# Numerator of the first half in SBUF, and y tiles grown one half at a time, in a fused attention and two-FFN kernel

## The chip, the cores and the metric

The kernel runs on one core of one Trainium2 chip. The metric is the device time of one execution in microseconds (us), lower is better; the figure for a kernel is the median of its runs.

## The reference

Attention over pooled keys and values, then a dense layer with a rational activation, then a routed layer in which each token goes to one of eight experts under a capacity limit:

```python
k_p = k.reshape(B, H, Sp, pool, D).mean(axis=3)          # pool = 8, Sp = 72
v_p = v.reshape(B, H, Sp, pool, D).mean(axis=3)
scores = scale * np.matmul(q, k_p.transpose(0, 1, 3, 2))
attn = softmax(scores)                                     # B = 8, H = 8, S = 576, D = 64
x = matmul(attn, v_p) as [4608 tokens, 512]
h = x @ w_in                                               # 512 -> 2048
P = a[0] + a[1] * h + a[2] * h2 + a[3] * h3
Q = 1.0 + np.abs(b[0]) * np.abs(h) + np.abs(b[1]) * h2
g = P / (Q + 1e-06)
y = g @ w_out                                              # 2048 -> 512
order = np.argsort(-(y @ w_gate).flatten())                # greedy: 576 tokens to each expert
out[mask] = np.maximum(y[mask] @ w1[e], 0.0) @ w2[e]       # 512 -> 1024 -> 512
```

## The kernel before

The 4608 tokens are 18 blocks of 256. Every float32 operand of a matmul is split into a high and a low part (`xh`/`xl`, `wih`/`wil`, `mg` high and low), and a product is three matmuls.

**Stages.** The dense layer is done in two halves of the 2048 hidden units. In the first half (`half` 0) attention is mixed in: units of scores (L560), softmax (L564 to L585), transposes (L595) and products with v (L613 to L616) make the next block's x while the blocks before it go through the dense layer. The second half (`half` 1) reads x back from DRAM. Then tokens are routed and the experts run (L1820 to L1863).

**A step.** One step is 256 hidden units of one block, or 128 hidden units of a pair of blocks: 512 columns in either case. There are 72 steps in each half. `mm_h` (L701) fills a PSUM bank `ph` with h. `act1` and `act2` work on 128x512 elements: ACT makes |h| (`ms`, L716), a3 h + a2 (`w`, L717) and the first term of Q (`q`, L719); DVE makes w h (L721) and then w = (w + a1) h (L722), POOL or DVE q |h|; ACT makes 1/Q by Ln and Exp (`mr`, L734 and L736). DVE then makes the high part of g (L737), a remainder `t` of it (L739, from q and the high part; L741, from w), and POOL the low part t/Q (L353, the line of a helper). In this kernel L722 writes w back into the bank `ph`, so that L737 and L741 read it there and the bank is held until L741 has ended.

**y.** `mm_y` multiplies g by `woh` and `wol` for one tile `tt` of 128 tokens. A tile is two PSUM banks, `g` = 0 and 1, of 260 columns each (256 of y, and 4 of the router's logits). The first tile of a part (all steps of one block or pair) grows step by step: after each step its matmuls go into both banks (L805 and L806 for the high part, L803 for the low). The other tiles are made when the part has all its steps, in `turn_y`. `y_out` then moves a finished tile out.

**Order.** PSUM has eight banks (`pa0` to `pa7`), which attention, `ph`, y and the preparation of weights share. Nothing is ordered by hand: each operation is recorded with an engine, a planned duration, what it reads and writes, and a list scheduler (`Order.run`) plays it through with the banks as a resource that is taken at an operation's start and freed when its last user ends. The order that comes out is the program, and each engine keeps to it. `w`, `q` have three buffers in turn (`mw`/`mq`, two of which are called `mwq` in the trace).

Of the kernel before, what the change touches and what calls it, by code (L numbers as in the profile page):

```python
# [18 lines left out]
ALU = mybir.AluOpType  # L19
# [4 lines left out]
B, H, S, D = 8, 8, 576, 64  # L24
# [7 lines left out]
NB = NT // BLK  # L32
# [266 lines left out]
class Kern:  # L299
# [408 lines left out]
    def act1(self, st):  # L708

        nc, op, i = self.nc, self.op, st["i"]  # L710
        ph = st["ph"]
        hk = [(ph, 0)]
        w, q, s = self.mw[i % 3], self.mq[i % 3], self.ms[i % 2]
        st["w"], st["q"] = ph, q
        N = 2 * BLK
        op("Act", c_act(N), lambda: nc.scalar.activation(s(), ph(), AF.Abs), r=hk, w=[s])  # L716
        op("Act", c_act(N, 0, 2), lambda: nc.scalar.activation(w(), ph(), AF.Identity, scale=self.a3(), bias=self.a2()),  # L717
           r=hk + self.sk, w=[w])
        op("Act", c_act(N, 1, 2), lambda: nc.scalar.activation(q(), s(), AF.Identity, scale=self.b1a(), bias=self.b0a()),  # L719
           r=[s] + self.sk, w=[q])  # L720
        op("DVE", c_tt(N), lambda: nc.vector.tensor_tensor(w(), w(), ph(), op=ALU.mult), r=hk, w=[w])  # L721
        op("DVE", c_stt(N), lambda: nc.vector.scalar_tensor_tensor(  # L722
            ph(), w(), self.a1(), ph(), op0=ALU.add, op1=ALU.mult), r=[w], w=hk)
        self.tt(N, q, q, s, ALU.mult, r=[s], w=[q])

    def act2(self, st):

        nc, op, i = self.nc, self.op, st["i"]
        w, q, r, t = st["w"], st["q"], self.mr[i % len(self.mr)], self.mt[i % MTB]
        hi, lo = g = self.mgl.pop(0)  # L730
        self.mgl.append(g)
        st["hi"], st["lo"] = hi, lo
        N = 2 * BLK
        op("Act", c_act(N, 1, 1), lambda: nc.scalar.activation(r(), q(), AF.Ln, scale=2.0 ** -LNS, bias=self.qcs()),  # L734
           r=[q], w=[r])
        op("Act", c_act(N, 1, 1), lambda: nc.scalar.activation(r(), r(), AF.Exp, scale=-1.0, bias=self.nls()), w=[r])  # L736
        op("DVE", c_stt(N), lambda: nc.vector.scalar_tensor_tensor(hi(), w(), self.a0(), r(), op0=ALU.add, op1=ALU.mult),  # L737
           r=[(w, 0), r], w=[hi])
        op("DVE", c_stt(N), lambda: nc.vector.scalar_tensor_tensor(t(), q(), self.qc(), hi(), op0=ALU.add, op1=ALU.mult),  # L739
           r=[q, hi], w=[t])  # L740
        op("DVE", c_stt(N), lambda: nc.vector.scalar_tensor_tensor(  # L741
            t(), w(), self.a0(), t(), op0=ALU.add, op1=ALU.subtract), r=[(w, 0), self.hring(st)], w=[t])
        self.tt(N, lo, t, r, ALU.mult, r=[t, r], w=[lo])

    def late(self, st):
# [34 lines left out]
        op("DVE", .12, lambda: nc.vector.tensor_tensor(lv(), pv(1), lv(), op=ALU.add), r=[pt], w=lk)  # L780
        self.keys(st["blks"][-1])

    def mm_y(self, st, tt):
        nc, op, fp = self.nc, self.op, st["fp"]
        _, _, woh, wol = self.w[st["half"], fp]
        hi, lo = st["hi"], st["lo"]
        late, two = self.late(st), len(st["cs"]) == 1
        if st["first"]:
            self.py[tt] = [Dyn(self.cls_f)] if late else [Dyn(self.cls_a) for _ in range(2)]
        py, c0, c1 = self.py[tt], st["cs"][0], st["cs"][-1]  # L790

        def mm(c, g, lower):
            o = 128 * tt + (0 if two else BLK * c)
            f = slice(o, o + 128)
            first, last = st["first"] and c == c0, st["last"] and c == c1
            if late:
                o = py[0]().rearrange("p (g d) -> p g d", g=2)
                w = lambda x: x()[:, c, :, 0:256]
            else:
                o = py[g]()[:, 0:GW]  # L800
                w = lambda x: x()[:, c, g, :]
            if lower:
                nc.tensor.matmul(o, lo()[:, f], w(woh), start=False, stop=last)  # L803
            else:
                nc.tensor.matmul(o, hi()[:, f], w(woh), start=first, stop=False)  # L805
                nc.tensor.matmul(o, hi()[:, f], w(wol), start=False, stop=False)  # L806

        ng = len(py)

        def wk(begin, end):  # L810
            if not two or late:
                return ["ybank", ("ybank", 1), ("ybank", 2)] if begin or end else []
            if tt == 0:
                return ["ybank"] if begin else [("ybank", 1)] if end else []
            if tt == 1:
                return [("ybank", 2)] if begin or end else []
            return ["ybank", ("ybank", 1), ("ybank", 2)] if begin or end else []
        for lower in range(2):
            for c in st["cs"]:
                ks = [(woh, k) for k in (c, 2 + c)] + ([] if lower else [(wol, k) for k in (c, 2 + c)])  # L820
                for g in range(ng):
                    wait = [st["part"][(Y0, Y1)[st["half"]]]["hi"]] if tt == 1 and two and not late and st["first"] and not lower else []
                    op("PE", ((.244, .122), (.458, .229))[ng == 1][lower], lambda c=c, g=g, lower=lower: mm(c, g, lower), r=[lo if lower else hi] + ks + wait,
                       w=[py[g]] + wk(st["first"] and c == c0 and not lower, st["last"] and c == c1 and g == ng - 1 and lower))

    def y_out(self, st, tt):
        nc, op, n, tb, tt = self.nc, self.op, st["blks"][tt // 2], tt, tt % 2
# [79 lines left out]
    def phase1(self):  # L907
# [61 lines left out]
        for h, ns, fs in parts:  # L969
            part = [dict(half=h, blk=ns[0], blks=ns, fp=f, cs=(0, 1) if len(ns) == 1 else (c,)) for f in fs for c in range(len(ns))]  # L970
# [5 lines left out]
        rest, held = [], []  # L976
        credit, closed = 0.0, False
        for i, st in enumerate(steps):
# [52 lines left out]
            else:  # L1031
# [13 lines left out]
                x = self.x1[turn % 2]  # L1045
# [29 lines left out]
            if not self.late(st):  # L1075
                held.append(st)
                if rest:
                    continue
                while held:
                    self.mm_y(held.pop(0), 0)  # L1080
                if st["last"]:
                    self.y_out(st, 0)
                    for tt in range(1, 2 * len(st["blks"])):
                        rest.append(lambda st=st, tt=tt: self.turn_y(st, tt))
                    rest.pop(0)()
# [5 lines left out]
        for i, n in enumerate(LATE):  # L1091
            part = next(self.parts[1, ns[0]] for ns in second if n in ns)
# [12 lines left out]

    def turn_y(self, st, tt):
        n = st["blks"][tt // 2]
        for x in st["part"]:
            self.mm_y(x, tt)
        self.y_out(st, tt)  # L1110
        if tt % 2:
            if st["half"] == 0 and n == SPLIT - 1 and st["fp"] < NFP - 1:
                self.load_yp(0)
            if st["half"] == 1:
                k = self.yorder.index(n) + 2
                if k < len(self.yorder):
                    self.load_ya(self.yorder[k])
# [383 lines left out]
    def route(self, k):  # L1501

        nc, V, rop = self.nc, self.nc.vector, self.rop
        D = lambda dur, fn, r=(), w=(), late=False: rop("DVE", dur, fn, r=r, w=w, late=late)
        L = lambda dur, fn, r=(), w=(): D(dur, fn, r, w, k > 0)
        tt, ts, stt = V.tensor_tensor, V.tensor_scalar, V.scalar_tensor_tensor
        last = k == E - 1
# [11 lines left out]
        K, BQ, ch, M, S2 = self.K, self.BQ, self.ch, self.M if k else self.Mb, self.S2  # L1519
        cq, cid, ra = self.cq, self.cid, self.ra  # L1520
        rk = lambda x: (self.rp, id(x))
        kk = lambda t, *a: [(t, n) for n in range(*(a or (NB,)))]
        c8 = (ch, 8)
# [28 lines left out]
        def ahead():  # L1552
            cw = lambda t, a, z: t().rearrange("p (g t) -> p g t", t=4)[:, a:z]
            wb = lambda n: self.wrb().unsqueeze(1).unsqueeze(3).to_broadcast([128, n, E, 4])
            for a, z, key in ((0, 8, rk(ch)), (8, 9, c8)):
                if a:
                    D(.1, lambda: ts(ch()[:, 8], self.R()[:, 8], 8.0, None, op0=ALU.is_equal), r=kk(self.R, NB - 2, NB), w=[c8])
                else:
                    D(.34, lambda: V.tensor_reduce(cq()[:, 0:8], K[0]().rearrange("p e g t -> p g t e"), op=ALU.max, axis=AX.X), r=[K[0]], w=[(cq, 0)])
                    own(a, z, key)  # L1560
# [16 lines left out]
        if not last:  # L1577
            if k == 0:
                J, jk = self.small(501, 5)
                D(.07, lambda: V.tensor_copy(J(), self.c("J")), r=[self.rc, *kk(self.R, NB - 2)], w=[jk])  # L1580
                D(.43, lambda: ts(ch()[:, 0:8], self.R()[:, 0:8], 8.0, None, op0=ALU.is_equal), r=kk(self.R, NB - 2), w=[rk(ch)])
                D(.06, lambda: V.memset(self.open8(), 1.0), r=[jk], w=[rk(self.open8)])
            spread(self.kq, BQ)

            def rest():
# [15 lines left out]
              r=[self.rc, (self.thr, 0)], w=[(T, 0), self.rj])  # L1601
            D(.15, lambda: ts(T()[:, E:2 * E], self.c("sel"), so(0)(), None, op0=ALU.mult, op1=ALU.add, accum_out=self.rj()),
              r=[self.rc, (self.sole, 0)], w=[(T, 1), self.rj])
            rop("PE", .2, lambda: nc.tensor.matmul(pt()[:, 0:2 * E], self.c("ones"), T(), start=True, stop=True),
                r=[(T, 0), (T, 1), self.rc], w=[pt])
# [378 lines left out]
```

## Time and profile before

| | before |
|---|---|
| median of 3 runs | 1502.45 us (1498.46 to 1506.28) |
| the profiled execution | 1500.95 us, span 1499.2 us |
| PE busy | 1451.5 us, 97% |
| DVE busy | 1077.9 us, 72% |
| ACT busy | 917.9 us, 61% |
| POOL busy | 877.0 us, 58% |

PE is TensorE, DVE VectorE, ACT ScalarE, POOL GpSimd, SP SyncE. PEld is the loading of a matmul's stationary operand, which runs beside PE. The time outside the span is 1.75 us. An engine is counted as busy while an instruction's record is open; matmuls overlap, so 97% for PE is no measure of how well it is fed. Times in the views run from the span's start. The first half lies between about 50 and 610 us, the second between 610 and 950.

### The profile page before, as it was taken

The numbers are of one execution on the slowest core, as the hardware profiler recorded it, in microseconds if no ns is written. First come the engines' busy times: TensorE is split into PE (matmuls) and PEld (weight loads), VectorE is DVE, ScalarE is ACT, GpSimd is POOL, SyncE is SP. The second block draws the span as 40 slices with busy tenths as digits, with TensorE's granted clock in tenths as the row PEclk, the third lists the DMA queues.
The fourth block names the chain that finished last, engine by engine and source line by source line (L and its number), as shares of the span: only waits on it lengthen the run. The fifth ranks groups of instructions, "written<-read, shape, count | busy, mean of one in ns | idle before, by whom it ended". The sixth has DMA issues, their size and how long they took to land. (4 is left out here: it accounts for less than half of the span.)

```text
span 1499.2 us, 27379 instructions
## 1 busy us (share of the span) xinstructions
PE 1451.5 (97%) x9516; PEld 1311.2 (87%) x9516; DVE 1077.9 (72%) x2909; ACT 917.9 (61%) x2203; POOL 877.0 (58%) x809
## 2 busy tenths in 40 slices
PE   8899999999999999999999999998999999999998
PEld 7899978888998999888999899766988988988997
DVE  6898787858678587897777877987878877831220
ACT  5887886868778686765446655842554543542431
POOL 5877887557666465764456554842465654653621
PEclk9999999999999999999999999999899999999999
DMA  6672543232422354531343333013254433433400
GB/s 218 221 238 99 168 144 131 80 113 89 144 99 71 103 153 126 166 82 63 111 113 85 85 97 102 1 47 126 86 173 141 152 113 118 155 121 99 140 26 32
DMA packets 109686, 173.62 MB, mean 116 GB/s; under 512 B 10336, under 2 KB 74208, under 8 KB 109536
## 3 DMA queue, kind: packets, MB, share of 16 engines
q1 hardware_dynamic: 84640, 134.02, 27.7%
q0 software_dynamic: 24896, 37.76, 9.1%
q8 instruction: 75, 1.23, 0.3%
q14 instruction: 75, 0.61, 0.1%
HBM read 122.29 MB, written 49.46 MB: 115 GB/s over the span
## 5 line engine op out<-in xcount | busy, mean ns | idle before, releaser
L701 PE MATMUL pa<-xh,wih 128*128 128x256 f32 (+1 forms) x576 | 202.3, 351 | 2.7 <-ACT ex L573 1.2
L701 PE MATMUL pa<-xh,wil 128*128 128x256 f32 (+1 forms) x576 | 195.4, 339 | 0.2 <-POOL wil L353 0.2
L701 PE MATMUL pa<-xl,wih 128*128 128x256 f32 (+1 forms) x576 | 195.2, 339 | 0.0
L353 POOL TENSOR_TENSOR mwq<-mwq,ms 128x512 f32<-128x512 f32 x96 | 130.2, 1357 | 97.4 <-ACT mwq L719 95.9
L716 ACT ACTIVATE ms<-pa 128x512 f32<-128x512 f32 x144 | 85.9, 596 | 113.0 <-PE pa L701 102.0
L1820 PE MATMUL pa<-yth,w1h 128*128 128x256 f32 (+1 forms) x512 | 146.0, 301 | 0.9 <-issue 0.7
L1820 PE MATMUL pa<-ytl,w1h 128*128 128x256 f32 (+1 forms) x512 | 144.9, 299 | 0.0
L1820 PE MATMUL pa<-yth,w1l 128*128 128x256 f32 (+1 forms) x512 | 144.8, 298 | 0.0
L353 POOL TENSOR_TENSOR mg<-mt,mr 128x512 fp32r<-128x512 f32 x75 | 96.9, 1292 | 61.1 <-DVE mt L741 43.2
L805 PE MATMUL pa<-woh,mg 128*128 128x260 f32 x480 | 125.5, 287 | 4.3 <-DVE mg L737 1.9
L806 PE MATMUL pa<-wol,mg 128*128 128x260 f32 x480 | 123.9, 284 | 0.0
L1873 POOL DMA_INDIRECT out<-ob,ix x40 | 39.0, 976 | 144.0 <-ACT ob L1869 116.0
L701 PEld LDWEIGHTS pa<-xh,wih 128*128 128x128 f32 x576 | 109.8, 191 | 14.5 <-ACT ex L573 2.0
L701 PEld LDWEIGHTS pa<-xh,wil 128*128 128x128 f32 x576 | 109.3, 190 | 13.1 <-POOL wil L353 0.4
L701 PEld LDWEIGHTS pa<-xl,wih 128*128 128x128 f32 x576 | 109.7, 190 | 9.1
L573 ACT ACTIVATE ex<-pa,nm 128x72 f32<-128x72 f32 (+2 forms) x320 | 98.6, 326 | 19.8 <-DVE nm L564 14.3
L741 DVE SCALAR_TENSOR_TENSOR mt<-pa,scal,mt 128x512 f32<-128x512 f32 x144 | 106.9, 743 | 1.3
L1823 ACT ACTIVATE h2h<-pa 128x256 fp32r<-128x256 f32 (+1 forms) x128 | 51.0, 407 | 84.9 <-PE pa L1820 79.5
L1854 PE MATMUL pa<-w2h,h2h 128*128 128x512 f32 x256 | 102.7, 401 | 0.0
L1854 PE MATMUL pa<-w2h,h2l 128*128 128x512 f32 x256 | 100.1, 391 | 0.0
L1828 DVE SCALAR_TENSOR_TENSOR h2l<-pa,h2h 128x256 fp32r<-128x256 f32 x128 | 53.7, 419 | 63.9 <-ACT h2h L1823 59.1
L1820 PEld LDWEIGHTS pa<-yth,w1h 128*128 128x128 f32 x512 | 95.9, 192 | 2.1 <-issue 1.5
(438 smaller groups left out, 4942.4 us busy)
## 6 DMA issues: line engine op xcount, KB each, us to landing
mwq<-in_w SPq DMA_DIRECT2D x42, 512.0 KB, 4.4
wraw<-in_w SPq DMA_DIRECT2D x22, 512.0 KB, 5.0
ya_d<-ya SPq DMA_DIRECT2D x18, 520.0 KB, 2.8
yab<-ya_d SPq DMA_DIRECT2D x18, 520.0 KB
kvraw<-in_kT SPq DMA_DIRECT2D x16, 576.0 KB, 4.2
x_d<-xh SPq DMA_DIRECT2D x18, 512.0 KB, 3.9
x_d<-xl SPq DMA_DIRECT2D x18, 512.0 KB
xh<-x_d POOLq DMA_DIRECT2D x18, 512.0 KB
```

The lines of the kernel that those rows point to most:

```text
L353: self.g.either({"Pool": (p_tt(n), lambda: nc.gpsimd.tensor_tensor(out(), x(), y(), op=alu)), "DVE": (c_tt(n), lambda: nc.vector.tensor_te ...
L573: op("Act", c_act(NK, 0, 1, 1), lambda h=h: nc.scalar.activation(e()[:n, h, :], sv()[:, h, :], AF.Exp, bias=nm()[:n, h:h + 1], accum_out=s ...
L701: nc.tensor.matmul(o, w()[:, c, f], x()[:, c].rearrange("p b t -> p (b t)") if two else x()[:, c, :], start=c == 0 and k == 0, stop=c == 3 ...
L716: op("Act", c_act(N), lambda: nc.scalar.activation(s(), ph(), AF.Abs), r=hk, w=[s])
L741: op("DVE", c_stt(N), lambda: nc.vector.scalar_tensor_tensor(t(), w(), self.a0(), t(), op0=ALU.add, op1=ALU.subtract), r=[(w, 0), self.hri ...
L805: nc.tensor.matmul(o, hi()[:, f], w(woh), start=first, stop=False)
L806: nc.tensor.matmul(o, hi()[:, f], w(wol), start=False, stop=False)
L1820: nc.tensor.matmul(ps()[:, 0:n], w()[:, c, fs], x()[:, c, :], start=i == 0, stop=i == 11)
L1823: fop("Act", c_act(n), lambda hh=hh, t=t, n=n, ps=ps: nc.scalar.activation(hh()[:, t], ps()[:, 0:n], AF.Relu), r=[ps], w=[(hh, half)])
L1828: fop("DVE", c_stt(t1 - t0), lambda hh=hh, o=o, o0=o0, ps=ps, t0=t0, t1=t1, half=half: nc.vector.scalar_tensor_tensor(o()[:, o0:o0 + t1 - ...
L1854: nc.tensor.matmul(ps(), x()[:, t], w()[:, f % 2, :], start=f == 0 and i == 0, stop=False)
L1873: fop("Pool", 1.05, lambda ob=ob, c=c, n=n: nc.gpsimd.indirect_dma_start(out=self.out, out_offset=bass.IndirectOffsetOnAxis(ap=ix()[:n, c: ...
```

## The change

Three edits.

1. In the first half, L722 writes its result into `w`'s own SBUF buffer and not into the bank `ph`; L737 and L741 read it from there. The last reader of the bank is then L722. In the second half nothing of this changes.
2. `mm_y` takes a list `gs` of halves. While a part's steps go by, the first tile's matmuls are issued for `g` = 0 alone; those for `g` = 1 follow for all steps after the last step. In `turn_y` all of a tile's `g` = 0 comes before its `g` = 1. This holds for both halves of the dense layer (not for the five last blocks of the second half).
3. Two operations of the routing get one more read key, which orders them behind the copy that takes the routing's bank.

```diff
         op("DVE", c_stt(N), lambda: nc.vector.scalar_tensor_tensor(
-            ph(), w(), self.a1(), ph(), op0=ALU.add, op1=ALU.mult), r=[w], w=hk)
+            (ph if st["half"] else w)(), w(), self.a1(), ph(), op0=ALU.add, op1=ALU.mult),
+           r=[w] if st["half"] else hk, w=hk if st["half"] else [w])
+        if st["half"] == 0:
+            st["w"] = w
...
-    def mm_y(self, st, tt):
+    def mm_y(self, st, tt, gs=(0, 1)):
...
-                for g in range(ng):
+                for g in gs[:ng]:
...
                 while held:
-                    self.mm_y(held.pop(0), 0)
+                    self.mm_y(held.pop(0), 0, (0,))
                 if st["last"]:
-                    self.y_out(st, 0)
+                    def other(st=st):
+                        for x in st["part"]:
+                            self.mm_y(x, 0, (1,))
+                        self.y_out(st, 0)
+                    other()
...
-        for x in st["part"]:
-            self.mm_y(x, tt)
+        for g in range(2):
+            for x in st["part"]:
+                self.mm_y(x, tt, (g,))
         self.y_out(st, tt)
...
-                    D(.1, lambda: ts(ch()[:, 8], self.R()[:, 8], 8.0, None, op0=ALU.is_equal), r=kk(self.R, NB - 2, NB), w=[c8])
+                    D(.1, lambda: ts(ch()[:, 8], self.R()[:, 8], 8.0, None, op0=ALU.is_equal), r=[(self.rp, 501), *kk(self.R, NB - 2, NB)], w=[c8])
```

The same number of instructions of each kind is issued on every engine. What moves is the order, because banks come free at other times. Line numbers after L722 grow by 3 at first: L737, L739 and L741 are L740, L742 and L744 after the change, L803, L805 and L806 are L806, L808 and L809.

The first place is PE in the first half, at about 340 us of the trace of before, where the step of `woh1`, `mg4` goes into the growing y tile, between transposes (`ident`, `en`) and scores (`kbd`, `qraw`) of attention. The name before the arrow is the bank. Before:

```order
L805 MATMUL pa4_231<-woh1_628,mg4_1458 128x260
L806 MATMUL pa4_231<-wol1_659,mg4_1458 128x260
L805 MATMUL pa5_233<-woh1_628,mg4_1458 128x260
L806 MATMUL pa5_233<-wol1_659,mg4_1458 128x260
L560 MATMUL pa0_130<-kbd0_100,qraw0_102 128x144 x2
L595 MATMUL pa2_194<-ident_115,en1_278 128x96 x3
L560 MATMUL pa3_197<-kbd1_112,qraw1_104 128x144 x2
L613 MATMUL pa1_148<-pth0_285,vmh0_120 128x192
```

After the change, at the same place:

```order
L808 MATMUL pa4_231<-woh1_628,mg4_1439 128x260
L809 MATMUL pa4_231<-wol1_659,mg4_1439 128x260
L560 MATMUL pa3_197<-kbd0_100,qraw0_102 128x144 x2
L560 MATMUL pa0_130<-kbd1_112,qraw1_104 128x144 x2
L701 MATMUL pa1_148<-xh0_353,wih2_998 128x512
L701 MATMUL pa1_148<-xl0_362,wih2_998 128x512
L701 MATMUL pa1_148<-xh0_353,wil2_1020 128x512
L613 MATMUL pa2_194<-pth0_285,vmh0_120 128x192
```

The y tile now takes one bank (`pa4`) where it took `pa4` and `pa5`, and h matmuls of the next step (L701, into `pa1`) stand between the scores and the products with v, where before only small attention matmuls stood. Nine more L701 rows of that step follow before the next step's L808.

The second place is DVE at the same step, whose h lies in `pa0`. Before:

```order
L737 SCALAR_TENSOR_TENSOR mg4_1458<-pa0_130,scal_93,mr0_835 128x512
L578 TENSOR_SCALAR sm2_400,junk_218<-sm2_400 96x4
L739 SCALAR_TENSOR_TENSOR mt1_990<-mwq1_766,scal_93,mg4_1458 128x512
L579 RECIPROCAL sm2_400<-sm2_400 96x4
L721 TENSOR_TENSOR mw_966<-mw_966,pa6_270 128x512
L741 SCALAR_TENSOR_TENSOR mt1_990<-pa0_130,scal_93,mt1_990 128x512
L722 SCALAR_TENSOR_TENSOR pa6_270<-mw_966,scal_93,pa6_270 128x512
```

After the change:

```order
L740 SCALAR_TENSOR_TENSOR mg4_1439<-mwq0_744,scal_93,mr0_835 128x512
L742 SCALAR_TENSOR_TENSOR mt1_1082<-mwq1_766,scal_93,mg4_1439 128x512
L578 TENSOR_SCALAR sm2_400,junk_218<-sm2_400 96x4
L744 SCALAR_TENSOR_TENSOR mt1_1082<-mwq0_744,scal_93,mt1_1082 128x512
L579 RECIPROCAL sm2_400<-sm2_400 96x4
L721 TENSOR_TENSOR mw_942<-mw_942,pa2_194 128x512
```

The bank `pa0` is no longer among the operands of L740 and L744: both inputs of each (`mwq0` and `mr0`, `mwq0` and `mt1`) are in SBUF, as both inputs of L739/L742 are in either kernel.

## Rows read from the trace of the kernel before

**Rows 1.** Busy time of each engine in five stretches; PEclk is the granted clock.

```profile
core 0: us, PE busy (x) PEld busy (x) DVE busy (x) ACT busy (x) POOL busy (x), PEclk, DMA share, GB/s
0.00:50.00 50.00, 44.27 (x340) 38.48 (x341) 32.38 (x88) 31.52 (x120) 32.27 (x52) 0.97 0.73 238
50.00:600.00 550.00, 530.94 (x3902) 496.25 (x3901) 430.01 (x911) 434.97 (x1257) 373.66 (x413) 0.99 0.41 128
200.00:250.00 50.00, 45.05 (x272) 39.06 (x271) 42.02 (x90) 36.95 (x111) 39.61 (x43) 0.97 0.34 109
300.00:350.00 50.00, 46.81 (x309) 41.78 (x308) 34.47 (x85) 37.25 (x128) 31.42 (x39) 0.97 0.33 104
700.00:850.00 150.00, 150.00 (x944) 135.69 (x943) 117.40 (x216) 91.39 (x142) 83.71 (x70) 1.00 0.32 89
```

**Rows 2.** Waits of PEld, 50 to 600 us: us in total, times, longest.

```profile
PEld pa L803 <- POOL mg L353: 3.6, 3, 1.8
...
PEld pa L560 <- DVE mt L741: 2.8, 4, 0.9
PEld pa L805 <- DVE mg L737: 2.6, 3, 1.8
PEld pa L805 <- DVE mt L741: 2.3, 3, 1.1
...
PEld pa L701 <- ACT ex L573: 2.0, 3, 1.4
PEld pa L595 <- POOL mq L353: 1.1, 2, 0.8
PEld pa L560 <- DVE xl L627: 1.1, 2, 0.7
PEld pa L805 <- DVE xl L627: 1.0, 1, 1.0
```

**Rows 3.** Timeline of DVE, 340 to 349 us: start, us, instruction.

```profile
340.61 0.74 DVE L741 SCALAR_TENSOR_TENSOR mt<-pa,scal,mt 128x512 f32<-128x512 f32 x1
341.27 0.74 DVE L722 SCALAR_TENSOR_TENSOR pa<-mw,scal,pa 128x512 f32<-128x512 f32 x1
...
348.48 0.73 DVE L741 SCALAR_TENSOR_TENSOR mt<-pa,scal,mt 128x512 f32<-128x512 f32 x1
```

**Rows 4.** Timeline of PE, 340 to 347 us.

```profile
340.45 0.28 PE L806 MATMUL pa<-wol,mg 128*128 128x260 f32 x1
341.41 0.76 PE L560 MATMUL pa<-kbd,qraw 128*128 128x144 f32 x4 [0.68 <-DVE mt L741]
...
346.58 0.39 PE L805 MATMUL pa<-woh,mg 128*128 128x260 f32 x1 [1.56 <-DVE mg L737]
```

**Rows 5.** Groups of DVE instructions, 50 to 600 us: busy us, mean ns, idle before.

```profile
L741 DVE SCALAR_TENSOR_TENSOR mt<-pa,scal,mt 128x512 f32<-128x512 f32 x70 | 51.9, 743 | 0.6
L737 DVE SCALAR_TENSOR_TENSOR mg<-pa,scal,mr 128x512 fp32r<-128x512 f32 x50 | 37.3, 746 | 20.8 <-ACT mr L736 15.4 <-PE pa L806 5.0
L739 DVE SCALAR_TENSOR_TENSOR mt<-mwq,scal,mg 128x512 f32<-128x512 f32 x34 | 36.7, 1080 | 1.4
...
L739 DVE SCALAR_TENSOR_TENSOR mt<-mq,scal,mg 128x512 f32<-128x512 f32 x16 | 18.1, 1130 | 0.6
```

**Rows 6.** Timeline of DVE, 289 to 294 us.

```profile
290.73 0.74 DVE L737 SCALAR_TENSOR_TENSOR mgx<-pa,scal,mr 128x512 fp32r<-128x512 f32 x1
...
291.99 1.32 DVE L739 SCALAR_TENSOR_TENSOR mt<-mwq,scal,mgx 128x512 f32<-128x512 f32 x1
```

**Rows 7.** Timeline of POOL, the same stretch.

```profile
289.64 1.30 POOL L353 TENSOR_TENSOR mgx<-mt,mr 128x512 fp32r<-128x512 f32 x1
291.47 1.28 POOL L353 TENSOR_TENSOR mwq<-mwq,ms 128x512 f32<-128x512 f32 x1 [0.52 <-ACT mwq L719]
```

**Rows 8.** Line L739: durations (min/median/max), who waited for it; whole span.

```profile
L739 DVE SCALAR_TENSOR_TENSOR mt<-mwq,scal,mg x57: 740/784/2414, 62.0 to 954.9; 128x512 f32<-128x512 f32 x57
...
  ACT mwq L719: 4.2, 4
```

**Rows 9.** Line L741: who waited for it; whole span.

```profile
  POOL mg L353: 54.8, 34
```

More of the change, by code (lines that the diff above doesn't have):

```diff
@@ L737, in act2 @@
         op("DVE", c_stt(N), lambda: nc.vector.scalar_tensor_tensor(hi(), w(), self.a0(), r(), op0=ALU.add, op1=ALU.mult),
-           r=[(w, 0), r], w=[hi])
+           r=[(w, 0), w, r], w=[hi])
         op("DVE", c_stt(N), lambda: nc.vector.scalar_tensor_tensor(t(), q(), self.qc(), hi(), op0=ALU.add, op1=ALU.mult),
@@ L741, in act2 @@
         op("DVE", c_stt(N), lambda: nc.vector.scalar_tensor_tensor(
-            t(), w(), self.a0(), t(), op0=ALU.add, op1=ALU.subtract), r=[(w, 0), self.hring(st)], w=[t])
+            t(), w(), self.a0(), t(), op0=ALU.add, op1=ALU.subtract), r=[(w, 0), w, self.hring(st)], w=[t])
         self.tt(N, lo, t, r, ALU.mult, r=[t, r], w=[lo])
@@ L787, in mm_y @@
         late, two = self.late(st), len(st["cs"]) == 1
-        if st["first"]:
+        if st["first"] and gs[0] == 0:
             self.py[tt] = [Dyn(self.cls_f)] if late else [Dyn(self.cls_a) for _ in range(2)]
@@ L820, in mm_y @@
                 ks = [(woh, k) for k in (c, 2 + c)] + ([] if lower else [(wol, k) for k in (c, 2 + c)])
-                for g in range(ng):
+                for g in gs[:ng]:
                     wait = [st["part"][(Y0, Y1)[st["half"]]]["hi"]] if tt == 1 and two and not late and st["first"] and not lower else []
                     op("PE", ((.244, .122), (.458, .229))[ng == 1][lower], lambda c=c, g=g, lower=lower: mm(c, g, lower), r=[lo if lower else hi] + ks + wait,
-                       w=[py[g]] + wk(st["first"] and c == c0 and not lower, st["last"] and c == c1 and g == ng - 1 and lower))
+                       w=[py[g]] + wk(st["first"] and c == c0 and not lower and g == 0, st["last"] and c == c1 and g == ng - 1 and lower))
     def y_out(self, st, tt):
@@ L1580, in route @@
                 D(.07, lambda: V.tensor_copy(J(), self.c("J")), r=[self.rc, *kk(self.R, NB - 2)], w=[jk])
-                D(.43, lambda: ts(ch()[:, 0:8], self.R()[:, 0:8], 8.0, None, op0=ALU.is_equal), r=kk(self.R, NB - 2), w=[rk(ch)])
+                D(.43, lambda: ts(ch()[:, 0:8], self.R()[:, 0:8], 8.0, None, op0=ALU.is_equal), r=[jk, *kk(self.R, NB - 2)], w=[rk(ch)])
                 D(.06, lambda: V.memset(self.open8(), 1.0), r=[jk], w=[rk(self.open8)])
```

## The prediction

> **What bounds the kernel now.** I first read the busy time by stretch, to see which engine has no time left. In 700 to 850 us, the second half of the dense layer, PE is busy for all 150 us [rows 1]: nothing that moves there can gain, and the new order of y tiles in that half can at best cost nothing. In 50 to 600 us, the first half with attention mixed in, PE is busy for 530.9 of 550 us [rows 1], so 19.1 us are open. [...] In the first 50 us, the start, PE's order is the same in both programs but for its last rows.
>
> Then I read who ends PE's waits in 50 to 600 us. I took the list of the weight loads, because a load stands ahead of its matmul and waits out the whole gap. Its rows fall into two kinds, which one tells apart by asking whether the waiting instruction reads what the other one wrote [rows 2]:
> - waits for a bank: a scores matmul (L560) or a y matmul (L805) does not read `t`, so its wait for L741 is a wait for the bank that L741 still reads: 2.8 and 2.3 us. Of the same kind are L701 behind the softmax, 2.0, and L560 and L805 behind `xl`, 1.1 and 1.0. Together 9.2 us, 5.1 of them by L741.
> - waits for data: L803 for the low part of g from POOL, 3.6, L805 for the high part from L737, 2.6, a transpose behind POOL, 1.1. Together 7.3 us.
>
> One place shows both. PE starts a matmul at 340.45 us and the next at 341.41, held 0.68 us by L741; it then runs small matmuls of attention, until at 346.58 it has waited 1.56 us more, this time for L737 [rows 4]. In between there was no h to compute, for want of a bank.
>
> **The change, part by part.**
>
> *The numerator in SBUF: what it frees.* In the step shown, L722 ends at 341.27 + 0.74 = 342.01 us and the L741 that reads the same bank (`pa6`; the first L741 of the group belongs to the step before) at 348.48 + 0.73 = 349.21 us [rows 3]. For these 7.2 us the bank is held for the numerator alone. Over 72 steps this is about 520 us of one bank in a stretch of 550: nearly one of eight banks on average. The waits of PE on L741 go: −5.1 us. I take them as gone entirely, since a hold that ends 7 us earlier is over before waits of at most 1.1 us begin [rows 2].
>
> *One half of the y tile.* While a part grows, one bank is taken where two were. This frees a second bank for most of the stretch; its price is that the `g` = 0 and `g` = 1 matmuls of the other tiles come one after the other, with the same count and shapes, so PE pays nothing. The output of a tile starts when both halves are done; its store is queued on SP a little later among the weight loads, and PE has no wait on that store among those of [rows 2]. Of the other bank waits, 9.2 − 5.1 = 4.1 us, I take half: −2.0 us. The bounds are 0, if these matmuls take the newly free banks only to wait for their data, and −4.1.
>
> *What the free banks do to waits for data.* In the order after the change twelve h matmuls of the next step stand among the attention matmuls where before there were none. PE then has something to do while DVE finishes g. Of the 7.3 us I take half, −3.6; bounds 0 and −7.3. [...]
>
> *What L737 and L741 cost from SBUF.* This is the part that speaks against the change. L737 and L741 now read one operand from PSUM and take 746 and 743 ns; L739, the same operation on the same size with both operands in SBUF, takes 1080 and 1130 ns in its two largest groups [rows 5], mean (34 × 1080 + 16 × 1130) / 50 = 1096. The reason shows in one place: L737 runs its 0.74 us from 290.73 while a POOL operation is open from 289.64 to 290.94, and loses nothing; L739 starts at 291.99 while one is open from 291.47 to 292.75, and takes 1.32 us, that is 0.56 us after POOL's end [rows 6, 7]. Left alone L739 takes 740, at worst 2414 ns [rows 8]. By this, L737 and L741 of the first half become like L739: +0.35 us each, the high part of g late by 0.35 and the low part by 0.70, and on DVE 72 × 0.70 = 50 us at most. The lower bound is 0; POOL sat idle for 34 of the L741s until they ended (54.8 us [rows 9]), and an idle POOL holds up nobody. I take 40 us: DVE goes from 430 [rows 1] to 470 of 550 us, 78% to 85%, so it keeps 80 us of slack and PE pays only where it stands waiting for g already. That is three times for the high and three for the low part [rows 2]: 3 × 0.35 + 3 × 0.70 = +3.2 us.
>
> [...]
>
> [...]
>
> *L722* keeps its one PSUM operand and writes to SBUF as L721 does: no price. *The routing's two read keys* order two short operations behind a copy on the same engine: nothing.
>
> Sum: −5.1 − 2.0 − 3.6 − 1.5 + 3.2 = −9.0 us. Against the profiled execution, 1500.95 (its span 1499.2 and 1.75 around it), this gives 1491.95. That execution lies 1.5 us under the median of the runs shown, 1502.45, so I put the median after the change at about 1493 us, 0.6% faster.
>
> **The rivals.**
>
> *DVE becomes what PE waits for (slower).* Place: L740, L742 and L744 follow each other closely in the new order, and each can meet a POOL operation; in 200 to 250 us DVE is busy for 42.0 of 50 us [rows 1] and every step there would add up to 0.70. For it: the softmax's small DVE operations queue behind these three. Against: 120 us of DVE are idle in the stretch. The gains are 5.1 + 2.0 + 3.6 + 1.5 = 12.2 us; it decides once 12.2 / 50, a quarter of the added DVE time, reaches PE. If half does, the time is 1500.95 + 25 − 12.2 = 1513.8, some 1515 as a median. [...]
>
> *The relief is eaten (no change).* A bank is free sooner but PE then waits for attention or for g, whose chain on ACT and DVE is no shorter. If a quarter of the DVE time reaches PE, 1501 to 1503. A variant with a place of its own: `w` has three buffers and each is now held until L744, so ACT's L717 three steps later may stop, with the softmax behind it. ACT waited 4.2 us in 4 times for L739 by the same ring of `q` [rows 8]. L741 ends 1 us or so after its L739, so the same four times cost some 4 us more, and if all of it reached PE the sum is −5 and the time 1497.
>
> [...]
>
> **How the numbers follow.** What a measurement of this kernel can tell from no change is about 0.5%, 7.5 us: 1495 to 1510. The forecast, 1484 to 1495, 0.42; attention runs through, 0.10; the relief eaten with its variant, 0.32; DVE as the bound, 0.16. So faster 0.52, same 0.32, slower 0.16. The range 1481 to 1511 holds the first three cases but for their edges and leaves out most of the last. The forecast's own range is 1484 to 1500.
>
> **What would show it.** Right: PE and PEld no longer wait on L744 in the first half; the waits of L560 shrink; L740 and L744 have means near 1.0 us, with L742 unchanged; DVE busy in 50 to 600 us near 470. The second half shows PE full in 700 to 850 as before. Wrong: waits of L806 and L808 on DVE and POOL grow by more than 9 us (DVE is the bound), L740 and L744 stay at 0.75 (no contention, and the forecast too slow), or PE's idle time stays near 19 us with other names in the list.

## The result, and the profile after

The change makes the kernel slower: 1519.90 us (median of 4 runs, 1519.38 to 1522.11) against 1501.84 for the kernel before in the same comparison, a ratio of 1.0121 with an interval of 1.0093 to 1.0150. That is 27 us above the predicted 1493 and 9 above the upper end of its range. The profiled execution took 1520.3 us, its span 1518.5. All of the loss lies ahead of the routing, and it is made in the first half. Counted by DVE's L722, one for each step, that of the 13th step starts 9.1 us later than before, that of the 37th 16.7, and those of the first and the last step of the second half 24.5 and 22.5 (610.2 and 991.9 us before, so the second half reaches further than 950). The last weight load of the dense layer's h starts at 977.8 us before and 999.5 us after, 21.7 later, so what follows it does not add to the loss. Its row gives min/median/max of its duration in ns and the first and last start; of before:

```profile
L701 PEld LDWEIGHTS pa<-xh,wih x576: 186/188/337, 42.2 to 977.8; 128*128 128x128 f32 x192
```

and of after:

```profile
L701 PEld LDWEIGHTS pa<-xh,wih x576: 186/188/337, 42.3 to 999.5; 128*128 128x128 f32 x192
```

Busy time by stretch, of the kernel after, to be held against [rows 1]:

```profile
core 0: us, PE busy (x) PEld busy (x) DVE busy (x) ACT busy (x) POOL busy (x), PEclk, DMA share, GB/s
...
50.00:600.00 550.00, 515.56 (x3711) 476.73 (x3709) 451.82 (x883) 419.09 (x1225) 381.45 (x403) 0.99 0.38 123
200.00:250.00 50.00, 44.86 (x273) 37.99 (x272) 45.47 (x95) 42.15 (x134) 41.48 (x44) 1.00 0.42 137
300.00:350.00 50.00, 49.80 (x341) 44.91 (x340) 37.85 (x73) 36.57 (x107) 31.88 (x36) 1.00 0.30 97
700.00:850.00 150.00, 150.00 (x973) 137.09 (x972) 117.37 (x229) 81.83 (x127) 79.98 (x65) 1.00 0.33 94
```

The second half shows PE busy throughout, as before. In 50 to 600 us PE is open for 34.4 us where it was open for 19.1, and gets through 3711 matmul records where it got through 3902. DVE is busy for 21.8 us more, although it too issues fewer instructions (883 for 911). In 300 to 350 us PE is busy for longer, 49.8 us for 46.8, and the clock went from 0.97 to 1.00, but this does not show that the place that the prediction looked at most closely has improved: the kernel after is 12 to 17 us behind by then, and the same stretch of time holds other steps. The step of [rows 3], the 36th, is followed below.

The waits of PEld in 50 to 600 us, of after, to be held against [rows 2]:

```profile
PEld pa L806 <- POOL mg L353: 11.9, 14, 1.8
PEld pa L808 <- DVE mg L740: 8.4, 10, 3.1
PEld pa L701 <- DVE xl L627: 4.1, 5, 1.5
...
PEld pa L806 <- POOL mgx L353: 2.7, 4, 1.5
```

No wait on L744 (L741 before) is left in the list. In its stead stand the waits for g itself: 11.9 + 8.4 + 2.7 = 23.0 us where [rows 2] had 3.6 + 2.6 = 6.2. A matmul of `woh` and `mg` does read what L740 and POOL write, so these are waits for data. They grew almost fourfold, and there are 28 of them (14 + 10 + 4) where there were six.

The groups of DVE in the same stretch, of after, to be held against [rows 5]:

```profile
L744 DVE SCALAR_TENSOR_TENSOR mt<-mwq,scal,mt 128x512 f32<-128x512 f32 x45 | 41.3, 919 | 0.4
L740 DVE SCALAR_TENSOR_TENSOR mg<-mwq,scal,mr 128x512 fp32r<-128x512 f32 x32 | 36.5, 1140 | 11.7 <-ACT mr L739 11.3
...
L742 DVE SCALAR_TENSOR_TENSOR mt<-mwq,scal,mg 128x512 f32<-128x512 f32 x32 | 33.0, 1030 | 1.6
```

L740 went from 746 to 1140 ns and L744 from 743 to 919; L742, which had both operands in SBUF already, stayed about where it was (1080 and 1030). How that looks at one place, the same 36th step that [rows 3] and [rows 4] show of the kernel before, is seen on DVE's timeline of after:

```profile
352.58 0.74 DVE L722 SCALAR_TENSOR_TENSOR mw<-mw,scal,pa 128x512 f32<-128x512 f32 x1
...
355.46 0.69 DVE L721 TENSOR_TENSOR mwq<-mwq,pa 128x512 f32<-128x512 f32 x1
356.06 4.65 DVE L740 SCALAR_TENSOR_TENSOR mg<-mw,scal,mr 128x512 fp32r<-128x512 f32 x1
360.64 0.54 DVE L627 SCALAR_TENSOR_TENSOR xl<-pa,xh 128x384 fp32r<-128x384 f32 x1
...
362.42 0.74 DVE L744 SCALAR_TENSOR_TENSOR mt<-mw,scal,mt 128x512 f32<-128x512 f32 x1
```

on POOL's:

```profile
354.30 1.91 POOL L353 TENSOR_TENSOR en<-ex,sm 96x256 f32<-96x256 f32 x4
356.16 1.83 POOL L534 TENSOR_TENSOR kvraw<-kvraw 128x768 f32<-128x768 f32 x1
357.95 1.26 POOL L353 TENSOR_TENSOR mwq<-mwq,ms 128x512 f32<-128x512 f32 x1
359.17 0.99 POOL L534 TENSOR_TENSOR kvraw<-kvraw 128x384 f32<-128x384 f32 x1
```

and on PE's:

```profile
357.40 0.49 PE L595 MATMUL pa<-ident,en 128*128 128x128 f32 x3
360.77 0.39 PE L808 MATMUL pa<-woh,mg 128*128 128x260 f32 x1 [2.88 <-DVE mg L740]
```

POOL has four pieces of work (four rows, the first of them four instructions) lined up without a gap, from 354.30 to 360.16 us. The L740 that DVE takes up at 356.06 is through 0.55 us after the last of them, having been open for 4.65 us instead of 0.75. DVE starts its next instruction at 360.64 us, so everything behind L740 in its order stands still for as long, and PE, which has used up its transposes, waits 2.88 us. Before the change PE waited 0.68 us for the bank and 1.56 us for L737 around this step [rows 4], and its L722 and L741 started at 341.27 and 348.48 us; now they (L722 and L744) start at 352.58 and 362.42. The wait for the bank is gone here, and the step is still longer by 2.6 us.

Such long ones are few. The row of L740 for this buffer, over the whole span:

```profile
L740 DVE SCALAR_TENSOR_TENSOR mg<-mw,scal,mr x17: 744/847/4653, 85.9 to 628.7; 128x512 fp32r<-128x512 f32 x17
```

Half of them take 847 ns or less, and a few of several microseconds raise the mean.

### The profile page after: what moved, and what is told of

It is laid out like the page before. It is cut to its first block, busy times and chain, and to the rows that moved or that the text cites. A ratio compares the mean times of both kernels' runs of the same rounds, so it can differ in the third digit from the quotient of the medians.

```text
span 1518.5 us, 27324 instructions
## 1 busy us (share of the span) xinstructions
PE 1455.8 (96%) x9516; PEld 1310.0 (86%) x9516; DVE 1120.5 (74%) x2909; ACT 918.3 (60%) x2203; POOL 901.0 (59%) x809
## 5 line engine op out<-in xcount | busy, mean ns | idle before, releaser
L701 PE MATMUL pa<-xh,wih 128*128 128x256 f32 (+1 forms) x576 | 202.5, 352 | 6.5 <-DVE xl L627 2.8
L701 PE MATMUL pa<-xh,wil 128*128 128x256 f32 (+1 forms) x576 | 194.8, 338 | 0.0
L701 PE MATMUL pa<-xl,wih 128*128 128x256 f32 (+1 forms) x576 | 194.6, 338 | 0.0
L353 POOL TENSOR_TENSOR mwq<-mwq,ms 128x512 f32<-128x512 f32 x96 | 135.5, 1412 | 84.1 <-ACT mwq L719 84.0
L353 POOL TENSOR_TENSOR mg<-mt,mr 128x512 fp32r<-128x512 f32 x75 | 98.6, 1316 | 72.9 <-DVE mt L744 58.3
L808 PE MATMUL pa<-woh,mg 128*128 128x260 f32 x480 | 131.8, 290 | 9.6 <-DVE mg L740 6.0
L809 PE MATMUL pa<-wol,mg 128*128 128x260 f32 x480 | 128.8, 284 | 0.0
L701 PEld LDWEIGHTS pa<-xh,wih 128*128 128x128 f32 x576 | 109.4, 190 | 18.8 <-DVE xl L627 4.1
L701 PEld LDWEIGHTS pa<-xh,wil 128*128 128x128 f32 x576 | 109.2, 190 | 12.6
L701 PEld LDWEIGHTS pa<-xl,wih 128*128 128x128 f32 x576 | 109.6, 190 | 9.0
L806 PE MATMUL pa<-woh,mg 128*128 128x260 f32 x480 | 106.0, 290 | 10.1 <-POOL mg L353 9.9
L737 ACT ACTIVATE mr<-mwq,scal 128x512 f32<-128x512 f32 x96 | 70.0, 729 | 59.3 <-POOL mwq L353 50.7
L353 POOL TENSOR_TENSOR en<-ex,sm 128x256 f32<-128x256 f32 (+5 forms) x160 | 85.6, 555 | 30.7 <-DVE sm L579 20.3
L808 PEld LDWEIGHTS pa<-woh,mg 128*128 128x128 f32 x480 | 91.0, 189 | 13.3 <-DVE mg L740 8.4
```

Source lines behind the costliest of these rows:

```text
L353: self.g.either({"Pool": (p_tt(n), lambda: nc.gpsimd.tensor_tensor(out(), x(), y(), op=alu)), "DVE": (c_tt(n), lambda: nc.vector.tensor_te ...
L701: nc.tensor.matmul(o, w()[:, c, f], x()[:, c].rearrange("p b t -> p (b t)") if two else x()[:, c, :], start=c == 0 and k == 0, stop=c == 3 ...
```

## The experiments

Two theories stood against each other. **A, the operands**: L740 and L744 now have two operands in SBUF, meet POOL there, and their lateness reaches PE. **B, the order**: the scheduler, given more banks, puts h matmuls ahead of work that PE needs sooner, and the DVE times are a side effect. The kernel before took 1501.64 us (17 runs) beside e1 to e4, 1502.63 (7 runs) beside e6a to e6d and 1502.53 (23 runs) beside e7 and e8; ratios are to these.

**e3_held: the numerator in SBUF, and nothing else.** The y edit is undone, and the plan still holds the bank `ph` until L744, so the order on PE is that of before but for 68 of some 4280 places.

```diff
-           r=[w] if st["half"] else hk, w=hk if st["half"] else [w])
+           r=[w], w=hk if st["half"] else [w, *hk])
...
-           r=[(w, 0), w, r], w=[hi])
+           r=[(st["ph"], 0), w, r], w=[hi])
```

> The plan of the kernel before (both y halves grow, the bank is planned as held until L741's counterpart), but the numerator is written to and read from SBUF. On PE 68 of some 4280 matmul places of the first half differ from the kernel before. Theory A (operands in SBUF meet POOL): the two operations grow from 0.745 to 0.95 to 1.15 us in the first half and the time is 15 to 25 us above before. Theory B (the new order is the cause): within 5 us of before, since the order is nearly the old one.

Measured: 1535.42 us (1534.22 to 1537.76), ratio 1.0218 (1.0193 to 1.0244). With nearly the old order and the bank held until L744, the two operands cost 33.8 us. Theory A had the durations about right and the time too low, by 8.8 us at the upper end of its 15 to 25. The DVE groups and then the waits of PEld in 50 to 600 us, of this kernel:

```profile
L744 DVE SCALAR_TENSOR_TENSOR mt<-mwq,scal,mt 128x512 f32<-128x512 f32 x44 | 41.9, 953 | 0.4
L740 DVE SCALAR_TENSOR_TENSOR mg<-mwq,scal,mr 128x512 fp32r<-128x512 f32 x31 | 35.7, 1151 | 10.4 <-ACT mr L739 10.3
```

```profile
PEld pa L808 <- DVE mg L740: 8.2, 7, 4.7
PEld pa L806 <- POOL mg L353: 7.9, 8, 2.3
```

If all 72 steps lengthen like the two groups, DVE gets 72 x (0.405 + 0.210) = 44 us more; 33.8 us, three quarters, arrive in the time of the kernel. B has no place here, since the order hardly differs. DVE's timelines show it too: of its 949 instructions up to 560 us before the change, 932 are found in the same order here. L722 itself, which now writes to SBUF, is no longer for it (741 for 748 ns in its largest group).

**e1_num: the numerator edit without the y edit.**

```diff
-                    self.mm_y(held.pop(0), 0, (0,))
+                    self.mm_y(held.pop(0), 0)
...
-        for g in range(2):
-            for x in st["part"]:
-                self.mm_y(x, tt, (g,))
+        for x in st["part"]:
+            self.mm_y(x, tt)
```

> Edit 1 alone: numerator in SBUF with its bank freed early, y tiles as before. Theory A: 5 to 20 us above before, a little better than with the bank held. Theory B: between before and after, depending on which edit makes the worse order; no forecast of the two operations' times.

Measured: 1521.28 us (1520.06 to 1523.06), ratio 1.0123 (1.0093 to 1.0152). From e3_held to this one only the plan's hold on the bank goes, and the time falls by 14.1 us: that is what the freed bank is worth in a kernel whose L740 and L744 are late. The time is within theory A's 5 to 20. What the bank would be worth without the lateness is not shown by these two.

**e2_y: the y edit without the numerator edit.** The diff is the y part of the change, on the kernel before, with the two read keys.

> Edit 2 alone: y tiles one half at a time, numerator in the bank. Theory A: not slower than before, 1490 to 1502 us, since no operand moves to SBUF. Theory B: 5 to 20 us above before.

Measured: 1499.84 us (1495.93 to 1501.45, 12 runs), ratio 0.9979 (0.9966 to 0.9992). A gain, as theory A had it, but of only 1.8 us. The waits of PEld in 50 to 600 us, of this kernel:

```profile
...
PEld pa L701 <- ACT ex L573: 3.8, 5, 1.3
PEld pa L560 <- DVE xl L627: 3.2, 3, 2.7
PEld pa L803 <- POOL mg L353: 3.0, 6, 1.2
```

The waits on L741 of [rows 2], 5.1 us, are 1.2 here in three rows of at most 0.6, but those behind the softmax and behind `xl` have grown from 2.0 and 1.1 to 3.8 and 3.2: PE meets the next wait. In the profiled execution the steps of the first half are no earlier than before (the 72nd and last L722 of it starts at 601.8 us, before at 599.5), so that what makes the small gain is open.

**e4_plan: the change, with the scheduler told the measured times.** If the lateness only surprises the plan, a plan that knows it should hide it.

```diff
-        op("DVE", c_stt(N), lambda: nc.vector.scalar_tensor_tensor(hi(), w(), self.a0(), r(), op0=ALU.add, op1=ALU.mult),
+        op("DVE", c_stt(N) + (0 if st["half"] else .4), lambda: nc.vector.scalar_tensor_tensor(hi(), w(), self.a0(), r(), op0=ALU.add, op1=ALU.mult),
...
-        op("DVE", c_stt(N), lambda: nc.vector.scalar_tensor_tensor(t(), q(), self.qc(), hi(), op0=ALU.add, op1=ALU.mult),
+        op("DVE", c_stt(N) + (0 if st["half"] else .35), lambda: nc.vector.scalar_tensor_tensor(t(), q(), self.qc(), hi(), op0=ALU.add, op1=ALU.mult),
```

(and 0.2 for L744.)

> The changed kernel, with the planner told longer times for the first half's three operations (0.40 us more for L740, 0.35 for L742, 0.20 for L744); the work is the same, the order is made anew. Theory A: PE's waits for g shrink, 1503 to 1512 us, and the two operations stay long. Theory B: no better than after, 1515 to 1525.

Measured: 1519.91 us (1516.38 to 1522.14), ratio 1.0119 (1.0088 to 1.0149), the time of the change as it was. My expectation was wrong. The waits of PEld in 50 to 600 us, of this kernel:

```profile
PEld pa L808 <- DVE mg L740: 6.3, 7, 3.5
PEld pa L806 <- POOL mg L353: 5.0, 6, 1.4
...
PEld pa L701 <- DVE mwq L722: 3.8, 3, 3.3
PEld pa L806 <- POOL mgx L353: 2.8, 4, 1.4
```

The waits for g shrank, from 23.0 to 6.3 + 5.0 + 2.8 (for `mgx`) = 14.1 us, and others took their place, such as h matmuls (L701) behind L722, the last reader of their bank. A plan with mean durations does not buy the lateness back.

**e6a to e6d: one order, four kinds of operand.** To tell A from B with the order fixed, the change is given seven PSUM banks, and the eighth holds a constant 0.5 that L740 and L744 name as an operand to wait for. e6a (the base) reads the numerator from SBUF as the change does. e6b reads the constant in PSUM instead, in both operations of the first half; e6c does so in L740 alone, e6d in L744 alone. In e6b to e6d the numerator is thus left out of those operations. The routing's work depends on the values, so whole times of e6b and e6d are not comparable; I compare the last start of an h load, before the routing. By the edits every engine gets the same instructions in the same order in all four, and DVE's timelines bear it out (all 947 instructions of e6b up to 560 us stand in the same order in the other three). Lines are 2 higher here (L742, L746, L703 for L740, L744, L701).

```diff
-        self.cls_a = DynClass(pa)
+        self.cls_a = DynClass(pa[:7])
...
+        self.still = pa[7]
+        self.op("DVE", .6, lambda: self.nc.vector.memset(self.still(), 0.5), w=[self.still])
...
-        op("DVE", c_stt(N), lambda: nc.vector.scalar_tensor_tensor(hi(), w(), self.a0(), r(), op0=ALU.add, op1=ALU.mult),
+        op("DVE", c_stt(N), lambda: nc.vector.scalar_tensor_tensor(hi(), (w if st["half"] else self.still)(), self.a0(), r(), op0=ALU.add, op1=ALU.mult),
```

(The first lines are the base; the last pair is the edit of e6c, and L744's is alike.)

> The changed kernel with seven banks in the plan; the eighth is filled once with 0.5 and not used. It is the base of the next three, which have the same instructions in the same order on every engine. Theory A: above after, 1520 to 1545 us, since a bank is missing. Theory B: the same.

> As the base with seven banks, but in the first half both operations read the constant bank in PSUM in place of the numerator (the numerator is left out of g there). Theory A (operands in SBUF meet POOL): both operations back to 0.745 us, and the time 25 to 35 us under the base. Theory B (the order is the cause): within 5 us of the base, since the order is the same.

> As the base with seven banks, but the first operation (high part of g) reads the constant bank in PSUM, the second (remainder) the numerator in SBUF. Theory A: the first back to 0.745 us, the second 0.9 to 1.1, the time 12 to 25 us under the base. Theory B: within 5 us of the base.

> As the base with seven banks, but the second operation (remainder) reads the constant bank in PSUM, the first (high part) the numerator in SBUF. Theory A: the second back to 0.745 us, the first 1.0 to 1.2, the time 5 to 15 us under the base, less than for the first operation since its lengthening is smaller. Theory B: within 5 us of the base.

Measured, the loads of h, with first and last start, of e6a:

```profile
L703 PEld LDWEIGHTS pa<-xh,wih x576: 186/188/337, 45.1 to 1019.5; 128*128 128x128 f32 x192
```

of e6b:

```profile
L703 PEld LDWEIGHTS pa<-xh,wih x576: 186/188/338, 44.8 to 983.3; 128*128 128x128 f32 x192
```

of e6c:

```profile
L703 PEld LDWEIGHTS pa<-xh,wih x576: 186/188/334, 45.0 to 994.7; 128*128 128x128 f32 x192
```

and of e6d:

```profile
L703 PEld LDWEIGHTS pa<-xh,wih x576: 186/188/337, 44.9 to 1001.2; 128*128 128x128 f32 x192
```

With the same order, where two operands lie makes 1019.5 − 983.3 = 36.2 us. Theory B falls. L744 alone from SBUF costs 994.7 − 983.3 = 11.4, L740 alone 1001.2 − 983.3 = 17.9; the two together cost 6.9 more than the sum. Each of these is one execution, and the whole times of e6c spread by 5.5 us, so that lateness is dearer where there is lateness already is suggested and not shown. Theory A's forecasts, against the base, were 25 to 35 us (36.2 by the loads), 12 to 25 (e6c, 24.8) and 5 to 15 (e6d, 18.3): the middle one held, the others were somewhat low, as was the base's 1520 to 1545. The DVE groups in 50 to 600 us, of e6a:

```profile
L746 DVE SCALAR_TENSOR_TENSOR mt<-mwq,scal,mt 128x512 f32<-128x512 f32 x44 | 42.4, 963 | 0.4
...
L742 DVE SCALAR_TENSOR_TENSOR mg<-mwq,scal,mr 128x512 fp32r<-128x512 f32 x31 | 33.2, 1071 | 11.6 <-ACT mr L741 11.4
```

and of e6b:

```profile
L746 DVE SCALAR_TENSOR_TENSOR mt<-pa,scal,mt 128x512 f32<-128x512 f32 x70 | 52.0, 743 | 0.7
...
L742 DVE SCALAR_TENSOR_TENSOR mg<-pa,scal,mr 128x512 fp32r<-128x512 f32 x50 | 37.3, 747 | 22.7 <-ACT mr L741 22.5
```

With one operand in PSUM L746 and L742 run at 743 and 747 ns. The waits of PEld for g in 50 to 600 us, of e6a:

```profile
PEld pa L810 <- DVE mg L742: 7.6, 7, 3.1
PEld pa L808 <- POOL mg L355: 7.4, 13, 1.5
...
PEld pa L808 <- POOL mgx L355: 1.7, 3, 1.1
...
PEld pa L810 <- DVE mgx L742: 1.2, 4, 0.4
```

and of e6b, where the last row is a scores matmul, which does not read g:

```profile
PEld pa L808 <- POOL mg L355: 4.0, 8, 1.7
...
PEld pa L562 <- DVE mgx L742: 0.2, 1, 0.2
```

The waits for g are 17.9 us in the one and 4.0 in the other. The whole time of e6c can be read, because what follows its last h load takes 526.7 us, as in e6a (525.8): 1521.42 us (1517.55 to 1523.04, ratio 1.0114, 1.0083 to 1.0145), beside e6a's 1545.31 (1542.97 to 1546.57, ratio 1.0276, 1.0246 to 1.0306): taking L740 alone out of SBUF gives 23.9 us, as against 24.8 by the loads. With seven banks and nothing late, e6b has its last h load 5.5 us after the kernel before with eight (977.8). So freed banks do buy time; how much they would buy with eight banks and no lateness was not run.

**e7_y_plan: the y edit, with L739 planned 0.30 us longer.** L739 has always had two operands in SBUF, and the plan counts it like the others.

```diff
-        op("DVE", c_stt(N), lambda: nc.vector.scalar_tensor_tensor(t(), q(), self.qc(), hi(), op0=ALU.add, op1=ALU.mult),
+        op("DVE", c_stt(N) + .3, lambda: nc.vector.scalar_tensor_tensor(t(), q(), self.qc(), hi(), op0=ALU.add, op1=ALU.mult),
```

> The y edit alone, with the planner told 0.30 us more for the operation whose operands were in SBUF all along (L739), in both halves: a try at a version under both kernels. Theory A (contention is the cost, and a plan that knows it helps where DVE has room): 1492 to 1499 us. Rival (a plan can't help, since the wait depends on where POOL stands): as the y edit alone, 1497 to 1502.

Measured: 1502.04 us (1499.09 to 1506.46, 12 runs), ratio 0.9996 (0.9979 to 1.0012). No gain, as in e4_plan; the rival's forecast of 1497 to 1502 held, theory A's did not.

**e8_y_first: the y edit in the first half alone.** The second half keeps the old order, and the numerator stays in the bank.

```diff
-                    self.mm_y(held.pop(0), 0, (0,))
+                    self.mm_y(held.pop(0), 0, (0, 1) if st["half"] else (0,))
...
-        for g in range(2):
+        for gs in ((0, 1),) if st["half"] else ((0,), (1,)):
             for x in st["part"]:
-                self.mm_y(x, tt, (g,))
+                self.mm_y(x, tt, gs)
```

> The y edit in the first half alone, the second half's y tiles as in the kernel before. If the small gain of the y edit comes from the first half: as the y edit alone, 1497 to 1502 us. If from the second half: as before, 1500 to 1505.

Measured: 1497.69 us (1494.76 to 1506.15, 12 runs), ratio 0.9970 (0.9954 to 0.9986). The time is the one forecast for a gain that comes from the first half. This version is under both kernels, by 0.3% to the one before. As in e2_y the first half's steps are no earlier (the 72nd L722 at 601.9 us). Its interval overlaps that of e2_y, so whether the second half's new order costs anything is not shown.

## Why the prediction was wrong, step by step

- *What bounds the kernel.* Right: from the last L722 of the first half to the last of the second it is 392.4 us in either kernel (599.5 to 991.9 and 622.0 to 1014.4), and the loss is made in the first half by what ends PE's waits. This says more than PE's busy time, of which the section on the profile before says that it is no measure of how well PE is fed.
- *The numerator in SBUF: what it frees* (−5.1). Right as a mechanism: the waits on L744 are gone entirely. The reading from one step holds too: the 72 holds from L722's end to L741's add up to 508 us in the trace of before, where 520 was estimated. Freeing the bank with all that follows from it is worth 14.1 us (e3_held to e1_num), in kernels that the late operands have slowed. The forecast had 12.2 for all gains with the y edit, 10.2 without its 2.0; the two are not quite the same thing, so that they lie close proves little.
- *One half of the y tile* (−2.0). Right in size by luck: −1.8 alone (e2_y), but not by the mechanism. The waits that it was to halve, those behind the softmax and behind `xl`, grew in e2_y, and its first half is no faster in the profiled execution. On top of the numerator edit it is −1.4 by the medians of e1_num and the change, whose runs overlap.
- *Waits for data* (−3.6). Wrong in sign: those for g grew by 16.8 us. They did so because of the term on L737 and L741 below, not by themselves: in e6b, whose L742 and L746 (L740 and L744) have one operand in PSUM, 4.0 us of them are left (6.2 before the change). The 1.1 us "behind POOL" did not belong here by the prediction's own question, since a transpose does not read `mq`; it weighs about 0.5 us in the sum.
- *The clock* (−1.5). No run shows this term: it was my own estimate, and the 1481 at the lower end of the range counts on it twice. What the traces show in its place, in windows of 1 us: of before, the granted clock is 0.50 from 242 to 244 and from 347 to 350 us; of after, 0.50 from 60 to 62, from 128 to 130 and from 380 to 383 us; in the rest of 50 to 600 us it is 0.99 to 1.00 in either, but for the windows next to these, at 0.54 to 0.98. So both stretches at 0.97 now show 1.00, but others are at 0.97 in their stead (50 to 100, 100 to 150 and 350 to 400 us), and the whole of 50 to 600 us shows 0.99 in either kernel: nothing was gained that the rows can show.
- *What L737 and L741 cost from SBUF* (+3.2). **This is the step that failed.** Its first part, on DVE, held roughly: +0.39 us for the one and +0.18 for the other by their largest groups, where +0.35 each was forecast. Its second part, the way from DVE to PE, was mis-sized tenfold: 33.8 us (e3_held) to 36.2 (e6a against e6b) and not 3.2. I charged the lateness at the six places where PE stood waiting for g already, and let 80 us of idle DVE absorb the rest. But the step's work is a serial chain, L740, L742, L744, POOL's low part, then PE; PE waits for g 28 times now, and 15 times in e3_held (its two rows) with nearly the old order, so the lateness reaches PE at many places where it had not waited. And the lateness does not come as 0.35 us at each step: a few of several microseconds, as at 356 us, are longer than what PE has to do meanwhile. That the long ones make most of the loss is argued from that one place and not measured.
- *DVE near 470.* 451.8 us in 50 to 600. The stretch now holds less of the work (883 instructions for 911), and L744 grew by half of what was forecast.

The path from the kernel before over e3_held and e1_num to the change is +33.8 − 14.1 − 1.4 = +18.3 us, and 18.1 was measured (1519.90 − 1501.84). The three are differences of successive kernels and must add up; the sum is no further evidence.

Of the rivals, *DVE becomes what PE waits for* is what happened. Its turning point was a quarter of the added DVE time reaching PE, and its price was worked out with a half; three quarters arrive (e3_held). With one operand in PSUM the largest groups of the two operations stay at 743 to 747 ns (before, e6b); with both in SBUF those of the first go to 1071 to 1151 and of the second to 919 to 963 (the change, e3_held, e6a). The *w-ring* variant is there but small: ACT's list has L717 waiting for L744 for 2.0 us, where some 4 were allowed for. That *the relief is eaten* is what the y edit alone shows. *Attention runs through*, the case above the forecast, did not occur.

Open: why the scheduler gains nothing from knowing the longer times (e4_plan, e7_y_plan), and what part of the loss goes by POOL, whose group `mwq<-mwq,ms` of L353 in 50 to 600 us went from 1323 to 1399 ns at the mean. The experiments show what the two operands in SBUF cost, POOL's part included. A kernel in which POOL does this work elsewhere, so that nothing meets, was not tried.

## What to carry to other kernels

Moving an operand from PSUM to SBUF is not only a question of banks; here it took L740 from 746 to 1140 ns. Ask what POOL has lined up at that moment, and price the move by a like operation that meets POOL already, by its longest ones as well as its mean (L739 before: 1096 and 2414 ns; L740 after: up to 4653). Then charge the added time along the whole serial chain, not just where the consumer already waits; DVE's idle share, 22% of 50 to 600 us before the change, was no cover here, where the work on it is a chain. And compare the same step in both traces, not the same stretch of time. Test the parts of such a change apart: here the small part (y in halves) was a gain on its own and the large one the loss.

## What the runs showed of the hardware that I had not expected

One DVE instruction with both operands in SBUF was open through several POOL instructions in a row, not only through the one that was open when it started: 4.65 us for 0.75, past the ends of POOL's rows at 356.2, 358.0 and 359.2 us, until 0.55 us after that at 360.16. POOL's rows follow each other without a gap there, and L740 is still open where each of them ends. It is no accident of one execution: the longest L742 for the same buffer takes 4.64 us in e6a, and none of the first half's takes more than 0.753 us in e6b, which has the same order and one of the operands in PSUM.

One bank of eight, taken away for the whole program (e6a against the change), costs this kernel 1545.31 − 1519.90 = 25 us, 20.0 of them by the last h load (1019.5 for 999.5).
